# Attention block on one core: output projections put off by up to five units, one and a half pairs per unit

## The chip, the core and the metric

One core of a Trainium2 chip runs the whole program. The metric is the device time in microseconds (us) of an execution. Executions of this kernel spread by 2 to 4 us within a set of runs, so medians of several runs are quoted. Ratios are the mean time of one kernel's fast runs over the mean of the other's fast runs of the same rounds, so not quite the ratio of the medians beside them.

The change begins at unit 16. So beside the medians I give, from each profile, the time **from the start of unit 16's scores to the end of the span**. It is a number from one execution, but free of the start.

## The reference

```python
B, Sq, D = 8, 112, 640;  H, Sk, Dh = 32, 512, 192      # all bf16
q = (x @ wq).reshape(B, Sq, H, Dh).transpose(0, 2, 1, 3)
scores = einsum("bhqd,bhkd->bhqk", q, k_cache) * Dh ** -0.5
p = softmax(scores)
o = einsum("bhqk,bhkd->bhqd", p, v_cache)
return o.transpose(0, 2, 1, 3).reshape(B, Sq, H * Dh) @ wo
```

## The kernel before

There are 64 units: 8 groups `g` of four heads, times 8 batch elements `b`. Unit `i` on TensorE is scores `S(i)`, transposes `T(i-2)`, slot 0, `PV(i-1)` (the product of the softmax weights with V), slot 1. The two slots of a unit hold projections: `("Q", g, c)` makes one block of 128 columns of a group's queries (ten matmuls, six blocks a group), `("O", g, m)` multiplies one block of 128 rows of a group's attention output with `wo` (twelve matmuls, seven blocks a group). Each writes two slices of `ps`, the program's tile in PSUM, hence "pair". A pair may be cut into a FRONT and a BACK part that stand in two slots. A table says what stands where:

```python
for g in range(NG):                                   # NG = 8
    i0 = 8 * g
    if g > 0 and g < NG - 1:
        put(i0, 0, ("O", g - 1, 4));  put(i0, 1, ("Q", g + 1, 0))
        put(i0 + 1, 0, ("O", g - 1, 5));  halves(i0 + 1, 1, ("Q", g + 1, 1))
        ...
        put(i0 + 5, 0, ("Q", g + 1, 4));  halves(i0 + 5, 1, ("Q", g + 1, 5))   # ends in slot 0 of i0 + 6
        put(i0 + 6, 1, ("O", g, 1))
        put(i0 + 7, 0, ("O", g, 2));  put(i0 + 7, 1, ("O", g, 3))
    ...
    else:                                             # the last group: no Q left
        halves(i0, 0, ("O", g - 1, 4));  halves(i0 + 1, 0, ("O", g - 1, 5))
        put(i0 + 2, 0, ("O", g - 1, 6), FRONT);  put(i0 + 3, 0, ("O", g - 1, 6), BACK)
        for m in range(4):
            halves(i0 + 4 + m, 0, ("O", g, m))
        ...
```

`halves(i, 0, p)` puts both parts of `p` into unit `i`; `halves(i, 1, p)` puts FRONT in slot 1 of `i` and BACK in slot 0 of `i + 1`. Waits on TensorE:

```python
def do_S(u):
    ...
    if b == 0 or u == 4:                     # first unit of a group: all its queries copied
        W(pe, aQ, q_index[g, 5, b // 4 if g == 0 else 1] + 1)
    W(pe, aEX, 4 * u)
    ...
def do_PV(u):
    ...
    W(pe, aT, u)                             # the transposes of unit u - 1 copied by ScalarE
    ...
def do_pair(i, j):
    ...
    steps = {FULL: range(n), FRONT: range(n // 2), BACK: range(n // 2, n)}[part]   # n: Q 5, O 6
    ...
def tevac(u):                                # ScalarE: that copy, into oT
    W(act, pT_, u + 1)
    if g > 0:                                # the O's that still read these columns
        W(act, pO, 2 * (MT * (g - 1) + (SQ * b + SQ - 1) // 128 + 1))
    ...
```

## Time and profile before

| | before |
|---|---|
| median of 3 runs (lowest, highest) | 394.29 us (393.0, 394.81) |
| span of the profiled run | 392.2 us |
| TensorE busy | 385.1 us, 98% |
| S of unit 16 to the end | 284.55 us |

The last row is one stretch of the profile (columns: stretch, length, then busy time of TensorE, its weight loads, the vector engine, ScalarE and GpSimd, then granted clock, DMA share, GB/s):

```profile
107.62:392.17 284.55, 280.48 (x6534) 178.74 (x6119) 211.94 (x381) 180.89 (x400) 105.48 (x237) 1.00 0.89 292
```

TensorE is idle for 4.07 us of it, 2.17 of them behind the last matmul, where no reordering helps; the next engine, the vector engine, is busy for 74%, and the DMA engines for 0.89.

### The profile page before, as it was taken

What the parts mean: (1) busy time and instruction counts of PE and PEld (TensorE: products, weight loads), DVE (VectorE), ACT (ScalarE), POOL (GpSimd) and SP (SyncE); (2) the same over time, 40 slices, a digit from 0 to 9 for tenths busy, and PEclk for the clock granted to TensorE, in tenths of its full rate; (3) what the DMA queues carried; (4) which work ended last, traced back from release to release, by engine and by line L of the source; (5) the groups of instructions that cost most, each with busy time, mean ns of one, the idle gap of its engine ahead of it and who ended that gap; (6) DMA issues with size and microseconds to landing.
All of it is one profiled execution on the core that took longest, in us unless ns stands there. A gap on an engine that the chain in (4) does not pass through costs nothing.

```text
span 392.2 us, 19832 instructions
## 1 busy us (share of the span) xinstructions
PE 385.1 (98%) x8833; PEld 242.8 (62%) x8286; DVE 283.2 (72%) x506; ACT 250.4 (64%) x550; POOL 152.8 (39%) x352
## 2 busy tenths in 40 slices
PE   8999989999999999999999999999999999998997
PEld 3556665665666666566566566666566666666664
DVE  1665687677777788786687676876678677789735
ACT  3767765776665774666755766566765766667562
POOL 5542553335433445135443255333354233234331
PEclk9999999999999999999999999999999999999999
DMA  8999999999999999899999899989999789989712
GB/s 264 376 371 368 342 325 337 355 349 344 337 317 330 356 336 330 290 301 345 325 329 297 268 321 360 326 277 315 286 344 296 222 299 300 352 278 313 251 39 70
DMA packets 88584, 120.00 MB, mean 306 GB/s; under 512 B 9776, under 2 KB 88496, under 8 KB 88496
## 3 DMA queue, kind: packets, MB, share of 16 engines
q1 hardware_dynamic: 88496, 118.72, 90.9%
q8 instruction: 68, 1.11, 1.2%
q14 instruction: 20, 0.16, 0.1%
HBM read 117.54 MB, written 1.15 MB: 303 GB/s over the span
## 4 chain that ended last, share of the span: by engine, by line
PE 96%; DMA 1%; issue 1%; DVE 0%; SPq 0%; ACT 0%
PE ps L933 22%; PE ps L972 22%; PE ps L858 22%; PE ps L954 21%; PE ps L983 6%; PE ps L892 2%; DMA wqs<-in_wq_dram 1%; PE ps L877 1%; SPq L1314 0%; PE ps L897 0%; PE ps L854 0%; DVE kt L1111 0%; DVE acc L1131 0%; ACT oT L1069 0%; ACT pT L1052 0%
## 5 line engine op out<-in xcount | busy, mean ns | idle before, releaser
L1111 DVE STREAM_TRANSPOSE kt<-kr 128x384 int32<-128x384 int32 x256 | 195.2, 871 | 12.0 <-DMA kr<-in_k_cache_dram 12.0
L1052 ACT ACTIVATE pT<-ps 128x448 bf16<-128x448 f32 x256 | 130.8, 561 | 84.6 <-PE ps L954 84.3
L954 PEld LDWEIGHTS ps<-qT,kt 32*128 32x128 bf16 x6144 | 77.1, 93 | 31.3 <-issue 23.7
L933 PE MATMUL ps<-wos,oT 128*128 128x320 bf16 (+2 forms) x342 | 93.2, 299 | 0.0
L972 PE MATMUL ps<-vm,pT 128*128 128x193 bf16 x768 | 91.5, 247 | 1.0 <-ACT oT L1069 0.8
L858 PE MATMUL ps<-wos,oT 128*128 128x320 bf16 x330 | 91.2, 299 | 0.0
L954 PE MATMUL ps<-qT,kt 32*128 32x112 bf16 x6144 | 87.5, 208 | 1.9 <-issue 1.7
L1231 POOL TENSOR_SCALAR bad<-rinv 112x4 f32<-112x4 f32 x64 | 14.6, 228 | 188.9 <-DVE rinv L1117 188.8
L1214 POOL COPY vm<-vs 128x1152 int32<-128x1152 int32 x64 | 73.5, 1148 | 25.4 <-issue 17.7
L972 PEld LDWEIGHTS ps<-vm,pT 128*128 128x128 bf16 x768 | 67.9, 97 | 22.1 <-ACT oT L1069 11.6
L933 PE MATMUL ps<-xT,wqs 128*128 128x448 bf16 x210 | 74.0, 352 | 0.0
L858 PE MATMUL ps<-xT,wqs 128*128 128x448 bf16 x210 | 73.9, 352 | 0.0
L1059 ACT ACTIVATE os<-ps,rinv 112x192 bf16<-112x192 f32 x128 | 47.8, 435 | 28.1 <-DVE rinv L1117 28.1
L972 PE MATMUL ps<-vs,pT 128*128 128x193 bf16 x256 | 62.6, 245 | 0.0
L933 PEld LDWEIGHTS ps<-wos,oT 128*128 128x128 bf16 x342 | 33.2, 97 | 43.1 <-issue 35.8
L1036 ACT ACTIVATE qT<-ps 128x448 bf16<-128x448 f32 x96 | 47.8, 554 | 18.8 <-PE ps L933 13.3
L1134 DVE TENSOR_TENSOR acc<-ps,acc 128x320 f32<-128x320 f32 x84 | 37.3, 486 | 27.1 <-PE ps L933 27.1
L1069 ACT ACTIVATE oT<-ps 128x672 bf16<-128x672 bf16 x64 | 46.4, 725 | 2.1 <-PE ps L983 2.1
L1117 DVE RECIPROCAL rinv<-ps 112x4 f32<-112x4 f32 x64 | 11.1, 174 | 48.7 <-PE ps L972 48.7
L933 PEld LDWEIGHTS ps<-xT,wqs 128*128 128x128 bf16 x210 | 20.4, 97 | 34.0 <-issue 28.9
L1120 DVE TENSOR_TENSOR os<-ps,rinv 112x384 bf16<-112x384 f32 x64 | 35.7, 558 | 7.4 <-DVE rinv L1117 0.5
L1207 POOL COPY wqs<-wqr 128x384 bf16<-128x384 bf16 x70 | 33.2, 507 | 4.8 <-DMA wqr<-in_wq_dram 4.8
(44 smaller groups left out, 154.6 us busy)
## 6 DMA issues: line engine op xcount, KB each, us to landing
kr<-in_k_cache_dram SPq DMA_DIRECT2D x256, 192.0 KB, 4.1
vs<-in_v_cache_dram SPq DMA_DIRECT2D x256, 192.0 KB, 4.0
wos<-in_wo_dram SPq DMA_DIRECT2D x48, 160.0 KB, 4.4
wqr<-in_wq_dram SPq DMA_DIRECT2D x35, 192.0 KB, 5.5
wqs<-in_wq_dram SPq DMA_DIRECT2D x5, 192.0 KB, 4.6
out_dram<-xs SPq DMA_DIRECT2D x6, 160.0 KB, 1.8
xs<-in_x_dram SPq DMA_DIRECT2D x2, 320.0 KB, 3.3
xs<-in_x_dram SPq DMA_DIRECT2D x1, 480.0 KB, 6.0
```

Source lines behind the costliest of these rows:

```text
L858: return pe.add_instruction(mybir.InstMatmult(name=nc.get_next_instruction_name(), engine=mybir.EngineType.PE, ins=[pe.lower_ap_or_imm(rhs ...
L933: mm = (pe.matmul if h == hs[0] and f == 0 else held)(ps[:, bank_of(pair, h), cs], w, rhs[h][:, cs], q == 0, q == n - 1 and f == cuts - 1)
L954: mm = pe.matmul(ps[:, a, SQ * t:SQ * (t + 1)], kt[u % NT][p, t, c // 2, :, c % 2], qT[g % 2][p, c, SQ * b:SQ * (b + 1)], start=(c == 0), ...
L972: mm = pe.matmul(pv[:, k, e, 0:DH + 1], pT[u % 2][:, a, t, :], src[:, a, v0:v0 + DH + 1], start=(t == 0), stop=(t == 3), skip_group_check= ...
L1036: act.activation(qT[g % 2][:, c, HQ * h:HQ * (h + 1)], ps[:, bank_of_Q0(n) if g == 0 else 6 + h, 0:HQ], ACTF.Copy).then_inc(aQ, 1)
L1052: act.activation(pT[u % 2][:, a, :, 0:SQ], ps[:, a, 0:4 * SQ].rearrange("p (t q) -> p t q", t=4), ACTF.Exp, scale=scale).then_inc(aEX, 1)
L1059: ins = act.activation(os_[u % 2][:, DH * (2 + e):DH * (3 + e)], pv_of(u)[0:SQ, 1, e, 0:DH], ACTF.Copy, scale=rinv[:, u % 4, 2 + e:3 + e])
L1069: act.activation(oT[:, :, SQ * b:SQ * (b + 1)].rearrange("p (k c) q -> p k c q", k=2), src.rearrange("p k (c q) -> p k c q", c=3), ACTF.Co ...
L1111: dve.transpose(dst, src).then_inc(vKT, 1)
L1120: dve.tensor_tensor(os_[u % 2][:, 0:2 * DH].rearrange("p (e d) -> p e d", e=2), pv[0:SQ, 0, :, 0:DH], rinv[:, u % 4, 0:2][:, :, None].broa ...
L1134: ins = dve.tensor_tensor(ob[:, m, cs] if g == NG - 1 else acc[:, m, cs], src, acc[:, m, cs], op=ALU.add)
L1214: gp.tensor_copy(vm[u % NM][:].rearrange("p a (t w) -> p a t w", w=RW)[:, :, :, 0:DH].bitcast(I32), vs[u % NV][:, :, 32:32 + 3 * DH].rearr ...
```

## The change

The intent is to even the load. Before, units 15, 16, 23, 24 and so on hold two pairs, and those of the last group one or a half. The change takes the pairs from unit 16 on from one stream that alternates O and Q while there are Q's, lets the O's fall behind by up to five units (O5.4 goes from unit 48 to 53), and so gives each unit from 16 to 61 one and a half pairs (units 48 and 55: two). Loads of `wo` move with it.

```diff
-        if g > 0 and g < NG - 1:
+        if g == 1:
...
-        else:
-            halves(i0, 0, ("O", g - 1, 4))
...
+    late = [("O", g, m) for g in range(1, NG) for m in range(MT)][4:]
+    stream = []
+    for g in range(2, NG - 1):
+        qs = [("Q", g + 1, c) for c in range(6)]
+        for n in range(7 if g == NG - 2 else 6):
+            stream += [late.pop(0)] + qs[n:n + 1]
+    stream += late[:-3]
+    counts = [3] * (NU - 16)
+    for i in (NU - 16, NU - 9):
+        counts[i - 16] += 1
+    for i in (NU - 2, NU - 1):
+        counts[i - 16] -= 1
...
+            if back:
+                put(i, j, back, BACK)
+                back, count = None, count - 1
+            elif count >= 2 and not (j == 0 and count == 2):
+                put(i, j, stream.pop(0))
+                count -= 2
+            elif count:
+                back = stream.pop(0)
+                put(i, j, back, FRONT)
...
+    wo_round = [0] + [8 * g - 1 for g in range(1, NG)]
+    for g in range(2, NG):
+        wo_round[g] = max(wo_round[g], 5 + max(i for (i, j), it in slot.items() if it and it[0] == ("O", g - 2, MT - 1)))
...
-                    d = u - (8 * g - 1)
+                    d = u - wo_round[g]
```

More of the change, by code (lines that the diff above doesn't have):

```diff
@@ L734, in build_main @@
             put(7, 1, ("O", 0, 3))
-        else:
-            halves(i0, 0, ("O", g - 1, 4))
-            halves(i0 + 1, 0, ("O", g - 1, 5))
-            put(i0 + 2, 0, ("O", g - 1, 6), FRONT)
-            put(i0 + 3, 0, ("O", g - 1, 6), BACK)
-            for m in range(4):
-                halves(i0 + 4 + m, 0, ("O", g, m))
-            put(i0 + 8, 0, ("O", g, 4))
-            put(i0 + 9, 0, ("O", g, 5))
-            put(i0 + 9, 1, ("O", g, 6))
+    late = [("O", g, m) for g in range(1, NG) for m in range(MT)][4:]
[10 more added lines that the diff above has]
+        counts[i - 16] -= 1
+    assert sum(counts) == 2 * len(stream)
+    back = None
+    for i, count in enumerate(counts, 16):
+        for j in range(2):
+            if back:
[7 more added lines that the diff above has]
+                put(i, j, back, FRONT)
+                count -= 1
+        assert count == 0
+    assert not stream and back is None
+    put(NU, 0, late[-3])
+    put(NU + 1, 0, late[-2])
+    put(NU + 1, 1, late[-1])
     pairs = [slot[i, j][0] for i in range(NU + 2) for j in range(2) if slot[i, j] and slot[i, j][1] != BACK]
```

## The prediction

> **What bounds the kernel now.** I read, in this order: the page's busy line, the chain of waits, a table of the stages between unit boundaries, the list of waits, then TensorE's timeline unit by unit. A "unit" is one pass of the main loop: scores S (96 matmuls), transposes T (6), slot 0, PV (16), slot 1. A slot holds a whole pair, a half pair or nothing; a pair is an output projection O (12 matmuls) or a query projection Q (10).
>
> Busy line and chain:
>
> ```profile
> PE 385.1 (98%) x8833; PEld 242.8 (62%) x8286; DVE 283.2 (72%) x506; ACT 250.4 (64%) x550; POOL 152.8 (39%) x352
> ...
> PE 96%; DMA 1%; issue 1%; DVE 0%; SPq 0%; ACT 0%
> ```
>
> TensorE is occupied for 385.1 of 392.2 us and is 96% of the chain. So a change helps only by removing idle TensorE time, and any wait it puts before a matmul goes straight to the end.
>
> The table of stages, cut where S of units 16, 24, 32, 40, 48, 56 and 63 starts (columns: stretch, length, busy time per engine with counts, clock, DMA share, GB/s):
>
> ```profile
> 107.62:155.00 47.38, 47.34 (x1090) 29.68 (x1018) 37.83 (x67) 30.64 (x68) 18.84 (x43) 1.00 1.00 334
> 155.00:202.11 47.11, 47.11 (x1090) 29.63 (x1019) 35.23 (x63) 30.63 (x68) 18.93 (x43) 1.00 0.96 317
> ...
> 296.33:343.45 47.12, 47.12 (x1090) 29.62 (x1019) 35.15 (x63) 30.63 (x68) 15.29 (x35) 1.00 0.90 291
> 343.45:378.01 34.56, 32.74 (x899) 22.86 (x863) 27.12 (x50) 22.21 (x49) 11.96 (x27) 1.00 0.76 242
> ```
>
> The middle is full. The idle time lies in 343.45 to 378.01, the last group, whose units hold half a pair or one. TensorE's timeline there shows what it is:
>
> ```profile
> 361.33 0.37 PE L954 MATMUL ps<-qT,kt 32*128 32x112 bf16 x13
> 362.88 1.21 PE L954 MATMUL ps<-qT,kt 32*128 32x112 bf16 x83 [1.18 <-issue]
> ...
> 367.58 0.37 PE L954 MATMUL ps<-qT,kt 32*128 32x112 bf16 x14
> 368.44 1.21 PE L954 MATMUL ps<-qT,kt 32*128 32x112 bf16 x82 [0.49 <-issue]
> ```
>
> Two scores stages break off after 13 and 14 matmuls for "issue": no engine is named. S of units 60 and 61 takes 2.69 and 2.00 us instead of 1.29: 2.1 us lost. Counting TensorE's records, weight loads included, the two gaps stand exactly 256 instructions apart. So I read them as instruction fetch, not as K, V or an exp.
>
> [...] its instruction queue has 68 packets for 1.11 MB, 16 KB each, and in the gaps the block's packet starts at 360.60 and 365.94 and ends about 1.3 and 1.5 us before work resumes. [...] So I use time between starts of stages, not the 98%.
>
> **Durations, each from start to start in TensorE's timeline.** S 1.293; T 0.306; PV 1.350; O in slot 0 1.632, in slot 1 1.724 (0.092 more because S follows); Q in slot 0 1.893, in slot 1 1.986; first two-fifths of a Q in slot 1 0.851, its last three-fifths in slot 0 1.137; half an O in slot 1 0.909; half an O in slot 0 1.008. That last is 0.192 over half of 1.632, and PV behind it 0.010 slower: PV waits until ScalarE has copied the last unit's transposes out. In the list of waits (waiter, releaser, total us, times, longest):
>
> ```profile
> PEld ps L972 <- ACT oT L1069: 11.6, 29, 1.0
> ```
>
> exp 0.54 then the copy 0.725 end 1.26 us after S; T plus half an O are over at 1.12. So a half O in slot 0 costs 0.20 us each time; three-fifths of a Q (1.137) does not. Before, eight units from 16 on have one (56 to 63), 1.6 us.
>
> **The change part by part.** Up to unit 15 nothing moves. I wrote the new slots out from the diff.
>
> 1. Units 16 to 47 repeat four kinds: O | Q front; Q back | O; Q | O front; O back | Q. By the row above: 1.293+0.306+1.632+1.350+0.851 = 5.432; 1.293+0.306+1.137+1.350+1.724 = 5.810; 1.293+0.306+1.893+1.350+0.909 = 5.751; 1.293+0.306+1.008+1.360+1.986 = 5.953. Sum 22.946; eight times 183.57 us.
> 2. Units 48 to 55: 6.57 (O | Q) + 5.432 + 5.810 + 5.751 + 5.953 + 5.432 + 5.810 + 6.566 (Q | O) = 47.32.
> 3. Units 56 to 61, one and a half O each: 5.490 and 5.691 three times = 33.54. Unit 62 as before 4.88, unit 63 to the end as before 14.16.
> 4. The sum is 283.47 us from S of unit 16 to the end; before it was 392.17 - 107.62 = 284.55. The 1.08 us gained is: 2.1 of fetch gaps removed, 0.25 of two small hitches in units 22 and 23, less six more half O's in slot 0 (fourteen against eight) at 0.20.
> 5. **A new wait.** S of the first unit of a group needs all of the group's queries copied out of PSUM (it waits for the last Q's second half). Before, the last Q ended in slot 0 of the unit two before, so this cost nothing. Now Q3.5, Q4.5, Q5.5 and Q6.5 (group, column block) stand whole in slot 1 of units 23, 31, 39 and 47, immediately ahead of S of 24, 32, 40 and 48. Only Q7.5, in slot 0 of 55, escapes. What such a wait lasts is readable where a Q already ends a unit, unit 8 of the kernel before:
>
> ```profile
> 66.60 0.35 PE L933 MATMUL ps<-xT,wqs 128*128 128x448 bf16 x1
> 66.79 0.35 PE L858 MATMUL ps<-xT,wqs 128*128 128x448 bf16 x1
> 66.99 0.98 ACT L1036 ACTIVATE qT<-ps 128x448 bf16<-128x448 f32 x2 [0.72 <-PE ps L933]
> 67.07 1.20 PEld L954 LDWEIGHTS ps<-qT,kt 32*128 32x128 bf16 x96 [0.56 <-issue]
> ```
>
> ScalarE's two copies end at 66.99 + 0.98 = 67.97; S, which there does not need them, starts at 67.07. With about 0.06 from ScalarE's end to TensorE's start (as PV shows behind the transposes' copy) S would start at 68.03: 0.96 us later. ScalarE is idle then: exps and norm are done some 0.5 us before. Four times 0.955 = 3.82 us, all on the path.
> 6. Wo's loads move from rounds 23, 31, 39, 47, 55 to 24, 33, 42, 52, 60, about five units ahead of first use, with 4.4 us to landing: hidden. Freeing of the attention-output buffer: every O ends at least a unit before its columns are overwritten. Vector engine: four K transposes about 0.74 apart (2.97), norm 0.76 and an O's copy 0.80 make 4.5 us a unit, 5.3 with two O's, under 5.4 and 5.7: hidden, with edges of 0.05 to 0.1 us.
>
> Together 284.55 - 1.08 + 3.82 = 287.29, or 2.7 us more. I add 0.1 for odd fetch gaps: 394.3 + 2.8 = 397.1 us.
>
> **The rivals.** (a) Balance wins: the light last group was starved, heavy units are relieved, and the time falls by 2 to 5 us (389 to 392). For: a DMA share of 0.76 at the end against 1.00 before[...]. Against: TensorE is full from 155 to 343, so pairs moved from there are added whole later; there is at most 2.1 + 1.6 + 0.25 us of idle to win, and step 5 stands in the program's order. Without step 5 the time would be 393.3. (b) Transfers become the bound: evened units at 22.946/4 = 5.74 us, with K and V of 1.57 MB and weights of 0.25 MB a unit, need 317 GB/s. Against: the kernel moved 355 GB/s from 13 to 60 us, and step 5 brings eight units to 22.946*2 + 0.955 = 46.85 us, nearly the old 47.11. If it failed: 399 to 403. (c) Fetch gaps move rather than go: blocks arrive 2.4 to 5.7 us after the previous is entered, and 256 instructions take some 5.5 us now; units 62 and 63 last 4.88 still. Worth 0 to 1 us. (d) Vector engine's copies late in units 57 to 61: 0 to 0.6 us.
>
> **Range and chances.** Step 5 is certain in kind and within 0.2 us each in size (3 to 4.6 us in all); the gain in step 4 holds to about 0.7; (c) and (d) lean upward; the runs of the kernel before spread 1.8 us. Eight in ten: 395.2 to 399.0. Two per cent is 386.4 to 402.2; under it there isn't enough idle time (chance 0.01); over it (b) would have to come true (0.03). Within: 0.96.
>
> **What would show it.** Right: S of units 24, 32, 40 and 48 starts about 1.2 us after the last Q matmul instead of 0.28, with waits on ScalarE's query copy; S of 60 and 61 takes 1.29; units 56 to 61 last 5.5 and 5.7 in turn; half O's ahead of PV take 1.01. Wrong: no wait at those four starts (then 393), waits of K transposes on K's loads in the middle (b), or gaps of "issue" in other S stages adding over 1 us (c).

The sum comes to 284.55 - 1.08 + 3.82 = 287.29 us from S of unit 16 to the end, and with 0.1 for odd gaps to 397.1 for the median.

- That the two breaks are instruction fetch is the author's estimate, and that they come where a unit lasts only 4.06 us (as 58 and 59 do in the trace) was said in a cut passage. What the trace of the kernel before shows: they stand at records 16065 and 16321 of TensorE, 256 apart, and end 1.31 and 1.48 us after a packet of the instruction queue ends. 68 packets of that queue go with 17178 records in the span, about 253 each. A **block** is here a stretch of 256 records that begins at such a place.
- The 2.4 to 5.7 us under (c) is an estimate from that trace: from a block's first instruction 0.1 to 3.4 us to the start of the next packet, about 1 us for the packet, 1.3 to its effect.
- "All on the path" in step 5 leaned on a cut rule about the order of matmuls. The changed kernel shows it for unit 32: no matmul starts from 202.46 to 203.69 us.

## The result, and the profile after

| | before | after |
|---|---|---|
| median of 6 runs (lowest, highest) | 394.31 us (393.0, 395.22) | 398.53 us (397.5, 400.32) |
| ratio of the fast runs | | 1.0112, 95% interval 1.0081 to 1.0143 |
| S of unit 16 to the end, profiled run | 284.55 us | 289.31 us |

The changed kernel is 1.1% slower, clear of the noise: within 2%, and inside the predicted range. Its busy line and chain of waits:

```profile
PE 386.3 (97%) x8833; PEld 242.3 (61%) x8286; DVE 285.4 (72%) x506; ACT 252.1 (63%) x550; POOL 152.7 (38%) x352
...
PE 94%; issue 2%; DMA 1%; ACT 1%; POOL 1%; DVE 0%; SPq 0%
```

ScalarE has entered the chain with 1%, and "issue" has gone from 1% to 2%. The stretch from unit 16 on:

```profile
107.93:397.24 289.31, 281.53 (x6534) 178.22 (x6119) 213.87 (x381) 182.03 (x400) 105.53 (x237) 1.00 0.88 287
```

The matmuls are the same 6534 and their busy time grew by 1.05 us; idle time of TensorE grew from 4.07 to 7.78 us. (In the loss of 4.76 us these two parts aren't sharply divided: the ends of matmuls are modelled, so the first 0.06 to 0.2 us of each wait count as busy.) Who ended TensorE's idle time in the whole run (waiter, releaser, total us, times, longest):

```profile
PE ps L979 <- ACT qT L1061: 3.6, 4, 0.9
...
PE ps L979 <- issue: 0.9, 1, 0.9
...
PE ps L958 <- issue: 0.8, 1, 0.8
```

The first row is new: four waits of scores on ScalarE's copy of the queries. This is one of them, at the start of unit 32 (start, length, engine, line, operation, idle time before):

```profile
202.27 0.35 PE L958 MATMUL ps<-xT,wqs 128*128 128x448 bf16 x1
202.46 0.35 PE L883 MATMUL ps<-xT,wqs 128*128 128x448 bf16 x1
202.66 0.98 ACT L1061 ACTIVATE qT<-ps 128x448 bf16<-128x448 f32 x2 [0.75 <-PE ps L958]
203.69 0.12 PEld L979 LDWEIGHTS ps<-qT,kt 32*128 32x128 bf16 x8 [1.51 <-ACT qT L1061]
```

From the second-last Q matmul to the copies' start is 0.39 us, as in unit 8 of the kernel before, where S did not wait; from the copies' end to S it is 0.05. S starts 1.23 us after the last Q matmul; without the wait it is 0.28.

The last group is mended, as intended. S of units 59 to 61, of which 60 and 61 had broken off before:

```profile
361.34 1.36 PE L979 MATMUL ps<-qT,kt 32*128 32x112 bf16 x96
367.03 1.36 PE L979 MATMUL ps<-qT,kt 32*128 32x112 bf16 x96
372.52 1.36 PE L979 MATMUL ps<-qT,kt 32*128 32x112 bf16 x96
```

But two such breaks now stand elsewhere, in S of unit 17 and between PV and Q of unit 24. (A break, or fetch gap, is idle time of TensorE in the midst of its work that no engine and no data transfer ended. The prediction reads it as a wait for the next block; that is a reading of the trace. These two stand at records 4801 and 6849, eight times 256 apart, and end 1.26 and 1.31 us after a packet of the instruction queue ends.)

```profile
113.36 0.43 PE L979 MATMUL ps<-qT,kt 32*128 32x112 bf16 x20
114.66 1.04 PE L979 MATMUL ps<-qT,kt 32*128 32x112 bf16 x69 [0.87 <-issue]
...
160.40 0.24 PE L997 MATMUL ps<-vs,pT 128*128 128x193 bf16 x1
161.43 0.36 PE L958 MATMUL ps<-xT,wqs 128*128 128x448 bf16 x1 [0.78 <-issue]
```

They cost 1.05 and 0.95 us, worked out as the stage's length less its usual one.

### The profile page after: what moved, and what is told of

It reads as the page before. It is cut to its first block, busy times and chain, and to the rows that moved or that the text cites. A ratio compares the mean times of both kernels' runs of the same rounds, so it can differ in the third digit from the quotient of the medians.

```text
span 397.2 us, 19832 instructions
## 1 busy us (share of the span) xinstructions
PE 386.3 (97%) x8833; PEld 242.3 (61%) x8286; DVE 285.4 (72%) x506; ACT 252.1 (63%) x550; POOL 152.7 (38%) x352
## 4 chain that ended last, share of the span: by engine, by line
PE 94%; issue 2%; DMA 1%; ACT 1%; POOL 1%; DVE 0%; SPq 0%
PE ps L997 22%; PE ps L958 21%; PE ps L979 21%; PE ps L883 21%; PE ps L1008 6%; PE ps L917 2%; DMA xs<-in_x_dram 1%; PE ps L902 1%; ACT qT L1061 1%; PE ps L879 1%; DMA vs<-in_v_cache_dram 0%; POOL vm L1239 0%; PE ps L922 0%; POOL wqs L1232 0%; DVE kt L1136 0%
```

## The experiments

Two theories stood at the start. Mine: the loss is the four waits on the query copy and the 0.2 us waits of more half O's, against which the fetch gaps of the last group are won back. The rivals: evening the units itself costs (K and V supply, late O's, late copies), or the gaps aren't fetch. All times "from unit 16" are from S of unit 16 to the end, of the profiled run.

| run | median us | ratio to before, 95% | from unit 16, us |
|---|---|---|---|
| before (runs of the same rounds) | 393.8 to 394.3 | | 284.55 |
| after | 398.53 | 1.0112 (1.0081, 1.0143) | 289.31 |
| 1 queries first | 397.34 | 1.0081 (1.0038, 1.0124) | 286.49 |
| 2 O's cut 4 and 2 | 395.75 | 1.0045 (1.0008, 1.0082) | 285.60 |
| 3 both | 395.30 | 1.0026 (0.9989, 1.0062) | 284.07 |
| 4 before, last group evened | 393.48 | 0.9988 (0.9948, 1.0028) | 282.96 |
| 5 order O Q O Q Q O, cut 4 and 2 | 392.08 | 0.9939 (0.9903, 0.9975) | 281.46 |
| 6 before, V loaded once | 391.98 | 0.997 (0.9917, 1.0023) | 282.38 |
| 7 after, V loaded once | 397.02 | 1.0077 (1.0033, 1.0122) | 287.31 |
| 8 before, 64 instructions more | 393.32 (one run) | | 282.69 |
| 9 before, last group evened and cut 4 and 2 | 392.08 | 0.996 (0.993, 0.999) | 280.92 |
| 10 order O Q O Q Q O alone | 392.44 | 0.9969 (0.994, 0.9998) | 282.40 |

All gave correct results but 6 and 7. Their outputs are wrong, which doesn't matter for the times.

**1. Queries first.** The last Q of a group then ends in slot 0 of the group's last unit.

```diff
-            stream += [late.pop(0)] + qs[n:n + 1]
+            stream += qs[n:n + 1] + [late.pop(0)]
```

> The changed kernel with one thing reordered: in the stream of units 16 to 55 each Q pair stands ahead of its O pair instead of behind it, so that the last Q of a group ends in slot 0 of the group's last unit and not in its slot 1. Counts per unit, number of half O's in slot 0 and wo's loads stay as they were. Theory (the wait of S for the copy of the last queries): S of units 24, 32, 40, 48 starts right behind the last matmul, 3.8 us come back, 398.5 becomes 394.7 (394 to 395.5). Rival one (evening the units itself costs, by K and V supply): stays at 398 to 399. Rival two (the late O's hold the path): stays, or gets slower, as the O's now stand half a pair later.

The four waits are gone: the list of waits has no row of scores on the query copy. But the median fell by 1.2 us only, not 3.8: a miss. (Nor did the rest stay quite as it was, as I had expected: there are fifteen half O's in slot 0 for fourteen, and two loads of `wo` start a unit later.) The trace shows two new kinds of wait. At the start of units 16, 24, 32, 40 and 48, a Q that now stands first waits 0.12 to 0.14 us for GpSimd's reordered weights. And in units 54 and 55, PV waits 1.05 us each. Unit 54 (last O matmul, ScalarE's copy of the transposes, PV):

```profile
330.67 0.30 PE L883 MATMUL ps<-wos,oT 128*128 128x320 bf16 x1
331.06 0.73 ACT L1094 ACTIVATE oT<-ps 128x672 bf16<-128x672 bf16 x1 [0.74 <-PE ps L883]
...
331.85 0.34 PE L997 MATMUL ps<-vm,pT 128*128 128x193 bf16 x2 [0.88 <-ACT oT L1094]
```

The copy overwrites columns of the attention output that O5.4 still reads (the second wait in `tevac`), and O5.4 now ends half a slot too late: O, then copy, then PV, one behind the other. That is a cost of late O's that the changed kernel itself just avoids. The theory of the four waits stands; the edit wasn't a clean test of its size.

**2. O's cut 4 and 2.** The larger part always goes to slot 0.

```diff
-                steps = {FULL: range(n), FRONT: range(n // 2), BACK: range(n // 2, n)}[part]
+                cut = n // 2 if k == "Q" else 4 if (part == FRONT) == (j == 0) else 2
+                steps = {FULL: range(n), FRONT: range(cut), BACK: range(cut, n)}[part]
```

> The changed kernel with halved O's cut 4 and 2 steps instead of 3 and 3, the 4 always in slot 0. Theory (PV behind a half O waits 0.2 us for ScalarE's copy of the transposes): four steps last 1.09 us, over the 1.01 needed, so the wait goes in all fourteen units, 2.8 us, 398.5 becomes 395.7 (395.2 to 396.5); waits at S of 24, 32, 40, 48 stay at 0.95 each. Rival (the 0.2 us is a cost of switching from O to PV, not a wait): no change, 398 to 399.

395.75, as expected. All fourteen waits are gone from the trace (in 52, 57 and the rest, PV follows at once), so they were waits for the copy and not a price of switching. Unit 57 in the changed kernel (the copy of the transposes, the last matmul of the half O, PV):

```profile
351.99 0.72 ACT L1094 ACTIVATE oT<-ps 128x672 bf16<-128x672 bf16 x1
...
352.44 0.30 PE L883 MATMUL ps<-wos,oT 128*128 128x320 bf16 x1
...
352.76 0.20 PEld L997 LDWEIGHTS ps<-vm,pT 128*128 128x128 bf16 x3 [0.50 <-ACT oT L1094]
352.77 0.43 PE L997 MATMUL ps<-vm,pT 128*128 128x193 bf16 x3
```

and here, where the last O matmul starts as the copy ends:

```profile
348.25 0.72 ACT L1095 ACTIVATE oT<-ps 128x672 bf16<-128x672 bf16 x1
...
348.97 0.30 PE L883 MATMUL ps<-wos,oT 128*128 128x320 bf16 x1
...
349.11 0.42 PE L998 MATMUL ps<-vm,pT 128*128 128x193 bf16 x3
```

From the last O matmul to PV it is 0.33 us there and 0.14 here. The four waits on the query copy stand at 0.95 to 0.99 as before.

**3. Both.**

> Both edits. Theory: the two costs lie in different places and add: 398.5 - 3.8 - 2.8 = 391.9 (391 to 393), under the kernel before by some 2.4 us (ratio 0.994), as then only fetch gaps are left. Rival (a floor elsewhere, as K and V supply at 1.57 MB in 5.7 us a unit): no lower than 394.

395.3, far from 391.9 and a second miss: the two new kinds of wait of run 1 are here again (1.05 us twice, 0.12 to 0.14 five times). The profiled run also lost some 4 us at unit 8, where nothing was edited: a Q waited 2.1 us for GpSimd's reordered weights, and behind that idle stretch its matmuls came 0.37 us apart instead of 0.19, with a mean clock of 0.996. From unit 16 it takes 284.07, 0.5 under the kernel before.

**4. The kernel before, last group evened.**

```diff
-            halves(i0, 0, ("O", g - 1, 4))
-            halves(i0 + 1, 0, ("O", g - 1, 5))
-            put(i0 + 2, 0, ("O", g - 1, 6), FRONT)
-            put(i0 + 3, 0, ("O", g - 1, 6), BACK)
+            slot[i0 - 1, 1] = None
+            for m in range(4):
+                halves(i0 + m, 0, ("O", g - 1, 3 + m))
```

> The kernel before with only its last group evened: O6.3 goes from unit 55 to 56, O6.4 to 57, O6.5 to 58, O6.6 to 59, so each of 56 to 63 holds one pair and lasts 4.88 us, none 4.06. Theory (the gaps in S of 60 and 61 are instruction fetch, because 256 instructions were used up in 4.1 us): the gaps go or fall under 0.5 us together, 394.3 becomes 392.2 (391.8 to 393). Rival (the end of the kernel waits for K or V, or for exp): the gaps stay near 2 us, 394.3.

S of 60 and 61 has no break, as the theory has it. (That is one execution; run 8 has hardly a break there either, with the last group as it was, so this alone does not show that evening removed them.) The median moved by 0.4 us only, within noise and not to the expected 391.8 to 393: a miss in size. The profile shows why it can be: a break of 0.62 us came up in unit 22 instead, and the saving from unit 16 was 1.59 us, not 2.1.

**5. The order O Q O Q Q O up to unit 47, and the cut of run 2.** Now only Q's are cut in the middle, the first unit of a group begins with an O, and its last Q ends in slot 0.

```diff
+        if g < NG - 2:
+            stream += [late.pop(0) if c == "O" else qs.pop(0) for c in "OQOQQO" * 2]
+            continue
```

> The changed kernel with two edits from unit 16 on: pairs of units 16 to 47 in the order O Q O Q Q O instead of O Q O Q O Q, so that only Q's are cut in halves there and the last Q of a group ends in slot 0; and the O's still cut further on are cut 4 and 2 steps. Units 48 to 55 keep the changed kernel's order (with the queries first, O5.4 and O5.5 came too late for the copy of the transposes, 1.05 us twice). Theory: neither the wait of S on ScalarE's query copy nor the 0.2 us ahead of PV is left; from S of unit 16 to the end it takes 280.7 us plus fetch gaps, 281 to 283 against 284.55 before; median 391 to 393 where before has 394, ratio 0.991 to 0.997. Rival (evened units bring something else, as K and V supply or late copies by the vector engine): 394 or more, with waits at K's transposes or ahead of O's.

392.08, ratio 0.9939: this version beats both kernels. Its stretch from unit 16:

```profile
109.31:390.77 281.46, 278.86 (x6534) 179.22 (x6119) 212.47 (x381) 180.16 (x400) 105.56 (x237) 1.00 0.89 294
```

TensorE is idle for 2.6 us of it: 2.17 behind the last matmul, as in every version, and most of the rest in two breaks that cost 0.63 and 0.18 us, in S of units 20 and 59.

**6 and 7. V loaded once.** V is loaded for units 0 to 3 only; the waits on its loads ask for those alone. Instructions on TensorE stay; only transfers go.

```diff
-                W(gp, mV[u % NV], 64 * (u // NV + 1))
+                W(gp, mV[u % NV], 64)
...
+                if u >= NV:                # load_v
+                    return
                 for a in range(4):
```

> The kernel before with V loaded for units 0 to 3 only and reused after that (wrong results on purpose), so nearly half of the data transfers are gone and every instruction stays. Theory (the gaps in S of units 60 and 61 are instruction blocks that wait behind data in the DMA engines): blocks start within 1 us of the previous block's entry instead of 0.1 to 3.4, the gaps are gone, S takes 1.29 everywhere from unit 16 on; 284.55 from S of 16 to the end becomes 282.3; the median also loses what the start wins. Rival (the gaps are waits for results of other engines): S of 60 and 61 still shows them.

The kernel before with that takes 282.38 from unit 16 and S of 60 and 61 is whole but for 0.04 us; one break of 0.12 is left, in unit 22. The detail about the blocks missed: counted in the trace, the time from a block's first instruction to the start of the next packet of the instruction queue fell only from 1.92 us (median of 46) to 1.29, not under 1.

> The changed kernel with V loaded once (wrong results on purpose). Theory: its fetch gaps in units 17 and 24 (1.05 and 0.95 us in the profiled run) go; the four waits of S on the query copy (0.95 each) and the 0.2 us of fourteen half O's stay, as they have nothing to do with transfers: 287.3 from S of 16 to the end, the 287.29 of the prediction's sum. Rival (part of those waits is transfers): it falls to that of the kernel before with the same edit.

This is the cleanest of the runs. The changed kernel without breaks:

```profile
107.60:394.91 287.31, 281.18 (x6534) 178.13 (x6119) 213.85 (x381) 182.01 (x400) 105.51 (x237) 1.00 0.52 160
...
PE ps L979 <- ACT qT L1061: 2.6, 3, 0.9
```

287.31 us is the prediction's 287.29. (The list names ScalarE three times; unit 24 waits 0.99 too but is put down otherwise.) Nearly halving what was moved from unit 16 on, 160 GB/s against 287, left all four waits and all fourteen waits of half O's: they have nothing to do with transfers. Runs 6 and 7 have hardly a break between them (0.2 us and under 0.1), so they show the cost of the change without breaks: 287.31 - 282.38 = 4.93 us, against 3.84 for the four waits and 1.2 for six more half O's. The breaks, 2.1 us of them in the profile before and 2.0 in the one after, add nothing to the loss of 4.76.

**8. 64 instructions more at the start.**

```diff
-    WARM, WN, BRIDGE, RAW = 5, 128, 3, 4
+    WARM, WN, BRIDGE, RAW = 2, 128, 3, 4
+            for j in range(67):
+                held(ps[:, 7, 0:8], wt[:], wt[:, 0:8], True, True)
```

> The kernel before with 64 more TensorE instructions ahead of the start (67 tiny warm-up matmuls in place of three large ones). Theory: blocks of 256 instructions begin 64 instructions earlier in the stream, so any break in TensorE that comes from fetch sits at instruction numbers of 1 modulo 256 (193 before) counted in the records, a few less where records are missing: in the last group behind S, not 13 matmuls into it. Rival: the breaks stay 13 and 14 matmuls into S of 60 and 61.

S of 60 and 61 is whole but for 0.08 us. Breaks came up elsewhere, 0.52 us between two O matmuls of unit 15, 0.26 in S of unit 30 and 0.17 in unit 57. Their number isn't 1 modulo 256, as I wrote, but 193 again. That expectation was an error of thought: with 64 instructions more ahead, the breaks still stand at 193 modulo 256 of the stream, and it is the program that moved by 64 against those places, so a break there meets an earlier point of the program. The other profiles agree on where breaks stand. From unit 8 to the end of unit 62 (but for unit 8 of run 3, where matmuls came 0.37 us apart), every break of over 0.34 us from one record's start to the next that no engine and no DMA ended stands at a number of 193 modulo 256, counted in TensorE's records (matmuls, weight loads and the 59 of its sequencer): 16065 and 16321 before, 4801 and 6849 after, 6849 in runs 2 and 10, 11713 in run 3, 6337 in run 4, 4289 and 5569 in run 5, 4545 in run 8. From profile to profile the breaks move from block to block, and none of these is off the blocks' edges. With one profile of each kernel it is not shown that the edits moved them.

**9. The kernel before, last group evened and cut 4 and 2.** Runs 2 and 4's edits; pairs up to unit 54 stay where they were.

> The kernel before with two edits in its last group only: one pair in each of units 56 to 63 (O6.3 to O6.6 one slot later each), and those O's cut 4 and 2 steps. Units 0 to 54 are untouched, so pairs of the middle aren't evened at all. Theory (TensorE is full in the middle, so evening it is worth nothing; all there is to win lies in the fetch gaps and the 0.2 us waits of the last group): 280.8 us from S of unit 16 to the end plus fetch gaps, 281 to 282; median 391 to 393, the same as the changed kernel with both its costs mended. Rival (evening the middle has a worth of its own): clearly slower than that one, 393.5 or more.

392.08 and:

```profile
108.17:389.09 280.92, 278.67 (x6534) 179.23 (x6119) 212.01 (x381) 181.07 (x400) 105.47 (x237) 1.00 0.90 296
```

The same median as run 5, which evens all units, and 0.5 us less from unit 16, as this execution met fewer breaks (0.3 us of them, and run 5 had 0.8): without them both come to 280.6. Run 9 was on another chip than run 5, so I compare the ratios: 0.996 and 0.994, with intervals that overlap. The part of the change that evens units 16 to 55 has no worth that these runs can see.

**10. The order alone.**

> The changed kernel with the order O Q O Q Q O in units 16 to 47 alone, halves left at 3 and 3 steps. Theory: the four waits of S on the query copy (3.85 us) and the eight 0.2 us waits of half O's in units 16 to 47 go, those six from unit 48 on (1.2 us) stay: 287.3 - 3.85 - 1.6 = 281.9 plus fetch gaps; median 392 to 394. Rival (the wait of S comes back elsewhere, as with the queries first): a new wait of about 1 us per group, 395 or more.

392.44; 282.40 from unit 16, of which 0.57 is one break in unit 24 (281.9 expected and 0.57 make 282.5). The list of waits has no row on the query copy, and no new wait in its place. So moving the four last Q's off the end of their groups takes back what run 1 only half showed. (The order also removes eight of the half O's, 1.6 us, so the whole gain is not that of the four waits.)

## Why the prediction was right

**Steps 1 to 3, the lengths of the units.** Apart from the breaks and the new waits, the four kinds came out at 5.43, 5.81, 5.75 and 5.95 us in every group, units 56 to 61 at 5.49 and 5.69 in turn, the end from unit 63 at 14.15. A stage took the same time in both kernels where the same stage followed, so lengths read from one kernel could be added up for another.

**Step 4, what is gained.** S of 60 and 61 is whole, and all fourteen half O's in slot 0 show their 0.2 us (0.18 in unit 23). Run 2 shows them to be a wait. But the gain itself, put at 1.08 us and said to hold to 0.7, did not come: without the four waits of step 5 the profile is still 0.92 us longer than before (289.31 - 3.84 - 284.55), as breaks of 2.0 us took the place of the 2.1.

**Step 5, the new wait.** Four times, at units 24, 32, 40 and 48: 0.99, 0.95, 0.95 and 0.95 us, 3.84 in all against 3.82 worked out. This was the mechanism that decided, and it was right. Run 10 shows that it is that placing which costs: with the order altered, waits of S are gone and no others come.

**Step 6.** Loads of `wo`, the vector engine and freeing of the attention output cost nothing in the changed kernel. Run 1 shows how near its edge the last one is: half a slot later, and two units lose 1.05 us each.

**The term that was too small** is "I add 0.1 for odd fetch gaps". The profiled run has 2.0 us of them from unit 16 on (units 17 and 24), and the median lies 1.4 us over the prediction, half a microsecond from the upper end of its range. How many breaks the five other runs had is not known. Rival (c) said that gaps would "move rather than go", and that is what happened; but its worth was given as 0 to 1 us. The prediction's own sign against it, gaps of "issue" in other S stages adding over 1 us, did appear: 1.05 us in S of unit 17. The prediction tied the gaps to units of 4.06 us. That fits the kernel before, where the late packets started 3.3 and 3.1 us after the block before them was entered; it left out packets that start later still: 4.1 and 4.2 us after, at the two breaks of the kernel after, in longer units. Before, units 16 and 24 held two pairs and lasted 6.57 us; now 5.43. In unit 16 the next block's packet starts 4.1 us after the block's first instruction (2.6 before), ends a microsecond later, and TensorE goes on 1.26 us after that: 6.5 us, more than such a unit lasts. That the shorter unit is to blame, and not only the longer wait for the packet, is argued and not shown; which blocks come late changes from run to run.

Rival (b), transfers as the bound, falls with run 7; rival (d), late copies by the vector engine in units 57 to 61, cost nothing, as these units have their worked-out lengths. Rival (a) mistook where idle time was. What could be won lay in the last group and at block edges, and run 9 wins 3.6 us in its profile (284.55 to 280.92) by touching the last group alone. Some of that is luck with breaks, of which it met 0.3 us: by the ratio of six runs, 0.996, it wins 1.6 us, what eight waits of 0.2 us come to.

## What to carry to other kernels

Evening the load between stages paid here only where TensorE, the engine that binds, had idle time (the last group, busy for 32.74 of 34.56 us: run 9, 0.996); in the middle, where it was busy for 47.11 of 47.11 us in a group, run 5 against run 9 (0.994 and 0.996) shows no gain from it. Before moving a producer, look for the consumer that waits for the last of a set, and leave the copy's time between them: here 1.23 us from the last Q matmul to scores, free in one slot and paid in the next. And look for breaks without a releaser whose places differ by multiples of 256 records: here they stood at 193 modulo 256, ended 1.3 to 1.5 us after a packet of the instruction queue (68 packets of 16 KB) in the profiles before and after, and cost 2.1 and 2.0 us there, 0.3 to 1.1 in the other profiles with all transfers, and at most 0.2 with V loaded once.
